# Attention with beacon keys and a gated MLP on one core: the order of work on every engine read from a table instead of made by a list schedule

## The chip, the cores and the metric

One core of a Trainium2 chip runs the whole program. Its engines are TensorE (PE, matrix products), VectorE (DVE), ScalarE (ACT), GpSimd (POOL) and SyncE (SP); each works through its own queue in order, and waits on semaphores for the others. Loads are issued from POOL, SP and ACT, stores from SP. The metric is the time of one execution on the device in microseconds. Before the change the median of 7 runs is 331.64 us (331.56 to 332.11).

## The reference

For 8 batches of 8 heads, 576 queries of width 64 attend to 16 beacon keys, which all may see, and to the keys up to their own place. The results of the 8 heads stand side by side as 4608 rows of 512, and go through an MLP of width 2048.

```python
k_all = np.concatenate([beacon_k, k], axis=2)
v_all = np.concatenate([beacon_v, v], axis=2)
scores = scale * np.matmul(q, k_all.transpose(0, 1, 3, 2))
causal[:, Nb:] = np.triu(np.ones((S, S), dtype=bool), k=1)
scores = np.where(causal, -1000000000.0, scores)
a = np.exp(scores - scores.max(-1, keepdims=True))
a /= a.sum(-1, keepdims=True) + 1e-09
attn_out = np.matmul(a, v_all)
x = attn_out.transpose(0, 2, 1, 3).reshape(B * S, H * D)
h = x @ w_in
out = (h * (1.0 / (1.0 + np.exp(-1.702 * h)))) @ w_out
```

## The kernel before

**Attention.** The work is cut into 16 sets, each of 4 heads of one batch. A set's queries and keys are loaded from POOL (`e_load_qk`, L373), its beacon keys from SP (`e_load_bk`, L408; for set 0 two of the four loads come from ACT) into one tile `bkf` that holds the beacon keys of all sets. VectorE casts a set's beacon keys (`e_bk`, L414, called `bk` and the set's number in the plan) and turns keys and queries with its 32 by 32 transpose (`e_turn`, L422 for the beacon part, L429 for the rest; `turn` in the plan). TensorE makes scores in chunks of 512 columns for 4 heads (`e_qk`, L458), all in one PSUM tile `s`, so that a chunk waits for the exp of the one before it (L469 on ScalarE). The causal edge is masked by POOL (L490), for the first two sets by VectorE (L483). Sums of the exps are taken by products with ones (`e_av` with x = 2, the sums product, L545; from set 4 on VectorE first adds the blocks up, `e_zadd`, L508), then transposed and inverted (L557, L564, L568: the "pair" z1 and z2), and the products with the values (L545, x = 0 and 1) are multiplied by the inverse into `xT` (`e_norm`, L580).

**MLP.** Rows come in groups: two of 256, eight of 512. The first product (`e_m1`, L604) fills one bank of 512 columns; the first two groups get their gate by tanh on ScalarE and a VectorE step (L618, L637), the others by one ScalarE step (L625), whose function table differs from exp's, so that ScalarE loads a table at each change. The second product of groups 2 to 9 is made of seven half-size products instead of eight (L718); VectorE prepares their operands (L669) and joins them (L734), and SP stores.

**Buffers.** Four PSUM banks form a ring for first products, second products and attention products. A bank is free again when the step that reads it (`closes`) has ended.

**Beacon loads after the first two sets.** The rest of `bkf` is filled in three parts, sets 2 and 3, 4 to 7, 8 to 15. For each part VectorE clears its slots (memset, L1086), and four loads on SP wait for that memset.

**The plan.** No instruction is issued where the code describes it. Each step is an `Op` with an engine, a length, and the ops that it depends on; `plan.run()` orders them, and the instructions are emitted in that order (L1103 to L1105). The program has semaphore waits for the true dependences, and no times: an engine does what is next in its queue as soon as its waits end. Before, `run` is a list schedule over those lengths: it takes the engine that can start first, and picks by priority, due time and a choice rule for TensorE (`choose`), with quotas for when a first-product group may start (`QUOTAS`), and due times for loads, turns and casts (`T_ATT0`, `T_ATT1`, `TDUE`). For a beacon load the plan counts 2500 ns from issue to landing:

```python
elif o.name == "bk" and o.eng != "DVE":
    lat = 2500
```

## Time and profile before

| | |
|---|---|
| median of 7 runs | 331.64 us |
| profiled execution | 331.86 us |
| its span, first to last instruction | 330.2 us |
| granted TensorE clock | 0.999 |
| TensorE busy | 311.1 us, 94% |
| VectorE, ScalarE, POOL busy | 237.9, 203.7, 115.5 us |
| first and last matmul | 8.60 us, 326.3 us |

The busy time of TensorE counts matmuls that overlap each other once. The strip below it in the page gives the busy share of 40 slices of 8.3 us. In the tables of groups and in the timeline, the number in brackets after an instruction is the time that its engine stood idle before it, and what ended that. Times that carry a "start to start" are differences between the starts of matmuls that follow each other.

### The profile page before, as it was taken

To read this page: it belongs to the slowest core of one execution; us is meant where nothing else is said; L and a number is where in the kernel's file an instruction comes from. 1 tells how busy PE (TensorE), PEld (TensorE's weight loads), DVE (VectorE), ACT (ScalarE), POOL (GpSimd) and SP (SyncE) were. 2 spreads that over 40 slices of the span, in tenths; PEclk is the share of its full clock that TensorE was granted. 3 is DMA by queue.
4 is the path that set the end of the run, shared out by engine and by line. 5 is a ranking of instruction groups with operands and counts; after the bars stand their busy time and mean duration, and the time that the engine had idled before them with its cause. 6 is when DMAs were issued, how large, how long until landed. Compare 5 with 4: busy or idle time off the path is not lost. (4 is left out here: it accounts for less than half of the span.)

```text
span 330.2 us, 9837 instructions
## 1 busy us (share of the span) xinstructions
PE 311.1 (94%) x4288; PEld 210.6 (64%) x4288; DVE 237.9 (72%) x478; ACT 203.7 (62%) x234; POOL 115.5 (35%) x178
## 2 busy tenths in 40 slices
PE   0699899999999999999999999999999999999995
PEld 0476566545885467646878877447774664746884
DVE  3847959796998788987999589978896630460484
ACT  1585487787767786777758586858677426175000
POOL 8765557372238205360427046702422000000000
PEclk9999999999999999999999999999999999999999
DMA  7999999669017903392149624930020000110122
GB/s 125 161 202 210 201 178 148 94 105 131 25 44 136 148 2 78 93 129 50 41 101 127 87 50 90 128 83 2 34 96 3 2 32 2 45 51 2 66 96 95
DMA packets 58219, 28.81 MB, mean 87 GB/s; under 512 B 41280, under 2 KB 53568, under 8 KB 58176
## 3 DMA queue, kind: packets, MB, share of 16 engines
q0 software_dynamic: 47552, 18.49, 48.1%
q1 hardware_dynamic: 10560, 9.69, 8.9%
q8 instruction: 33, 0.54, 0.7%
q14 instruction: 10, 0.08, 0.1%
q10 hardware_dynamic: 64, 0.01, 0.0%
HBM read 37.22 MB, written 9.44 MB: 141 GB/s over the span
## 5 line engine op out<-in xcount | busy, mean ns | idle before, releaser
L604 PE MATMUL u<-xT,w 128*128 128x512 f16 (+1 forms) x704 | 130.5, 342 | 2.4 <-DVE g L637 1.1
L469 ACT ACTIVATE E<-s 128x2048 f16<-128x2048 f32 (+4 forms) x66 | 98.8, 1514 | 42.8 <-PE s L458 42.1
L604 PEld LDWEIGHTS <-w 128*128 128x128 f16 x704 | 67.6, 98 | 59.1 <-issue 3.7
L625 ACT ACTIVATE g<-u 128x512 f16<-128x512 f32 x128 | 74.4, 599 | 43.2 <-PE u L604 43.1
L490 POOL TENSOR_SCALAR_AFFINE_SELECT E<-E 128x512 f16<-128x512 f16 (+3 forms) x78 | 50.7, 672 | 120.5 <-ACT E L469 116.8
L734 DVE SCALAR_TENSOR_TENSOR osb<-u,osb 128x512 f32<-128x512 f32 x56 | 37.4, 679 | 40.5 <-PE u L718 26.9
L718 PEld LDWEIGHTS <-g 128*128 128x128 f16 x512 | 48.7, 98 | 7.3 <-issue 0.2
L458 PE MATMUL s<-qT,kT 32*128 32x32 f16 (+20 forms) x1376 | 35.7, 234 | 12.0 <-DVE qT L429 8.6
L718 PE MATMUL u<-w,g 128*128 128x256 f16 x384 | 46.0, 273 | 0.0
L458 PEld LDWEIGHTS <-kT 32*128 32x128 f16 x1376 | 26.1, 95 | 29.0 <-issue 14.8
L718 PEld LDWEIGHTS <-sA 128*128 128x128 f16 x384 | 36.4, 98 | 4.9
L718 PE MATMUL u<-tB,sA 128*128 128x256 f16 x256 | 31.3, 273 | 0.0
L389 POOL DMA_DIRECT2D vb<-in_v_dram x32 | 27.3, 870 | 2.9 <-DMA kn<-in_k_dram 1.5
L545 PE MATMUL u<-E,vb 128*32 128x352 f16 (+8 forms) x928 | 27.7, 267 | 0.0
L580 DVE TENSOR_TENSOR xT<-u,rz 128x352 f16<-128x352 f32 (+2 forms) x52 | 24.8, 517 | 1.7 <-PE u L545 1.1
L508 DVE TENSOR_TENSOR zs<-zs,E 128x1344 f16<-128x1344 f16 (+2 forms) x36 | 23.2, 645 | 2.7 <-DVE zs L508 0.5
L545 PEld LDWEIGHTS <-vb 128*32 128x32 f16 (+1 forms) x928 | 20.1, 98 | 5.4 <-issue 1.3
L429 DVE STREAM_TRANSPOSE kT<-kn 128x576 f32<-128x576 f32 x16 | 20.1, 1258 | 4.7 <-PE s L458 2.8
L429 DVE STREAM_TRANSPOSE qT<-qn 128x576 f32<-128x576 f32 x16 | 20.0, 1247 | 3.7 <-DMA qn<-in_q_dram 1.9
L669 DVE TENSOR_TENSOR sA<-g 128x512 f16<-128x512 f16 x32 | 12.8, 417 | 12.4 <-ACT g L625 12.0
L557 DVE STREAM_TRANSPOSE zt<-u 128x352 f32<-128x352 f32 (+2 forms) x32 | 13.8, 459 | 7.8 <-PE u L545 7.6
L718 PE MATMUL u<-tB,g 128*128 128x256 f16 x128 | 16.3, 273 | 0.0
(44 smaller groups left out, 229.6 us busy)
## 6 DMA issues: line engine op xcount, KB each, us to landing
out_dram<-osb SPq DMA_DIRECT2D x36, 256.0 KB, 2.2
kn<-in_k_dram POOLq DMA_DIRECT2D x16, 288.0 KB, 6.3
qn<-in_q_dram POOLq DMA_DIRECT2D x16, 288.0 KB, 6.7
vb<-in_v_dram POOLq DMA_DIRECT2D x24, 128.0 KB, 5.6
w<-in_moe_w_in_dram POOLq DMA_DIRECT2D x8, 256.0 KB, 9.5
w<-in_moe_w_out_dram POOLq DMA_DIRECT2D x4, 512.0 KB, 14.0
vb<-in_v_dram POOLq DMA_DIRECT2D x8, 112.0 KB, 3.6
vb<-in_v_dram POOLq DMA_DIRECT2D x8, 80.0 KB, 5.4
```

The source lines that it names most:

```text
L389: nc.gpsimd.dma_start(out=t[0 : hi - lo, j, h0:h1, :], in_=v[b, h0:h1, lo:hi, :].rearrange("h n d -> n h d"),)
L429: nc.vector.transpose(out=f32(dst.rearrange("p n e -> p (n e)")).rearrange("p (r t) -> p t r", t=TR), in_=f32(src[:, :]).rearrange("p (t c ...
L458: nc.tensor.matmul(sc[:, h, o : o + w], kT[s % NB2][r : r + 32, j * P : (j + 1) * P, d], qT[s % NB2][r : r + 32, a : a + w, d], start=(d = ...
L469: nc.scalar.activation(out=Es[s][:, :, c0:c1], in_=ss[i][:, :, o : o + c1 - c0], func=AFT.Exp, scale=0.125,)
L490: nc.gpsimd.affine_select(out=blk, in_=blk, compare_op=ALU.is_ge, fill=0.0, base=off + (Nb if j == 0 else 0), pattern=[[0, Q], [1, w]], ch ...
L508: nc.vector.tensor_tensor(out=t, in0=E[:, :, Z0:S] if i == 1 else t, in1=E[:, :, wcol[i] : wcol[i] + S - a], op=ALU.add,)
L545: nc.tensor.matmul(u[32 * h : 32 * h + 32, a:e], lhs, src[0:kw, h, col : col + e - a], start=first, stop=last,)
L580: nc.vector.tensor_tensor(out=xT[:, 2 * hs + x : 2 * hs + x + n, t0 : t0 + w], in0=rings[("av", s, x, half)][:, 0 : n * w].rearrange("p (n ...
L604: nc.tensor.matmul(u[:, o + a - t0 : o + e - t0], w1t[:, kp, nt * P : (nt + 1) * P], xT[:, kp, a % XR : (e - 1) % XR + 1], start=(kp == 0) ...
L625: nc.scalar.activation(out=gts[g][:, n0:n1, 0:w], in_=rings[("m1", g, n0)][:, 0 : n * w].rearrange("p (n w) -> p n w", n=n), func=AFT.Gelu ...
L718: nc.tensor.matmul(u[:, HM * mt : HM * (mt + 1)], lhs[:, n, mt * P : (mt + 1) * P], rhs[:, n, :], start=(n == 0 and mt == 0), stop=(n == H ...
L734: nc.vector.scalar_tensor_tensor(out=osbs[(g, dst)][:, :], in0=rings[("p", g, p)][:, :], scalar=scale_of(g), in1=osbs[(g, src)][:, :], op0 ...
```

## The change

The list schedule is gone, with its rules, quotas and the two constants `NEAR` and `IDLE`. In its place stands a table `ORDER` with one row for each engine and one for the DMA queue of POOL: the numbers of the ops, in the order in which they were described in the code, written down in the order in which the engine is to do them. `run` takes each row from its head, and works out starting times from the same kind of lengths and latencies, only to assign ring banks and to emit the rows in one common order. Due times and priorities are still written at the ops, and nothing reads them any more. Some dependences are added to the plan (a transpose of sums waits for the inverse two before it; VectorE's additions wait for the sums products two sets before; a tanh waits for the tanh before it and for a gate three before); they name buffers that are reused. The planned length of VectorE's additions goes from 0.517 to 0.6 ns per element. The ops themselves, what each issues, are as before.

The table is cut here to the heads of four rows. In them 73 and 97 are the beacon casts of sets 0 and 1; 74 and 75 the turns of set 0's keys and queries, 98 and 99 those of set 1; 82 is the memset for sets 2 and 3, 83 to 86 are its four loads, 224 is the cast of set 2, and 225 and 226 are its turns; 126 and 128 are norms of set 0's second half; on TensorE 76, 100, 106, 108 are score chunks 0 to 3, 145 the sums product of set 1's second half, 176 the first step of a second product.

```diff
-NEAR = 500
-IDLE = 800
+ORDER = {
+    "PE": [
+        76, 100, 115, 118, 120, 106, 138, 143, 141, 108, 152, 111, 155, 158, 129, 161, 122, 164, 131, 167, 170, 134,
+        127, 125, 173, 176, 145, 148, 150, 177, 182, 188, 191, 227, 194, 197, 183, 232, 203, 200, 234, 178, 179,
...
+    "DVE": [
+        73, 97, 74, 75, 98, 99, 78, 81, 80, 116, 117, 102, 121, 104, 105, 119, 139, 140, 144, 142, 154, 157, 123,
+        124, 82, 160, 166, 163, 169, 172, 224, 126, 128, 175, 146, 147, 149, 151, 225, 226, 87, 190, 193, 196, 255,
...
+    "SP": [
+        0, 2, 4, 5, 6, 7, 83, 84, 85, 86, 88, 89, 90, 91, 181, 93, 94, 95, 96, 187, 217, 223, 348, 364, 371, 377,
...
     def run(self):
-        free = {e: 0 for e in ("PE", "ACT", "DVE", "POOL", "Q", "SP")}
+        todo = {e: [self.ops[i] for i in seq] for e, seq in ORDER.items()}
+        free = {e: 0 for e in todo}
         free.update(POOL=900, SP=700)
...
+        while any(todo.values()):
+            n = len(order)
+            for e, seq in todo.items():
+                k = 0
+                for o in seq:
+                    if any(d.end is None for d in o.deps):
+                        break
+                    t = max([free[e]] + [d.end + self.lat(d, o) for d in o.deps])
...
+                    o.start, o.end = t, t + dur
+                    free[e] = o.end
+                    order.append(o)
+                    k += 1
+                del seq[:k]
...
+    def lat(self, d, o):
+        if o.eng == "Q":
+            return 300 if d.eng == "SP" else 1200
+        if d.name == "bk" and d.eng != "DVE":
+            return 2500
+        return self.LAT[d.eng] if o.eng != d.eng or d.eng == "Q" else 0
...
-    QUOTAS = (19, 28, 38, 42, 48, 55, 55, 55)
...
-    T_ATT0, T_ATT1 = 17000, 249000
+    T_ATT0, T_ATT1 = -1000, 245000
...
+            deps += [avs.get((s - 2, 2, h)) for h in range(2)] if s - 2 >= EARLY else []
...
-    SQ, SDVE, TDUE = 2, 0, 60000
+    SQ, SDVE, TDUE = 2, 0, 75000
```

## The prediction

> **What bounds the kernel now.** I read the page first, then the stretch-by-stretch table, the list of waits, the timeline of the first 14 us and the view of the beacon-key tile `bkf`.

> ```profile
> PE 311.1 (94%) x4288; PEld 210.6 (64%) x4288; DVE 237.9 (72%) x478; ACT 203.7 (62%) x234; POOL 115.5 (35%) x178
> ...
> PE   0699899999999999999999999999999999999995
> ```

> TensorE is the bound: one empty slice at the start, one half-empty at the end, nearly full between. It starts its first matmul at 8.60 us and ends its last at 326.3; a join and a store close the span of 330.2. So a new order can win only what TensorE stands still. Where that is, stage by stage (PE busy is the first number after the length):

> ```profile
> 33.00:66.00 33.00, 31.29 (x582) 19.85 (x584) 25.77 (x45) 22.70 (x22) 18.23 (x30) 1.00 1.22 155
> 66.00:99.00 33.00, 32.54 (x435) 21.30 (x428) 28.82 (x54) 24.99 (x28) 13.71 (x19) 1.00 0.55 76
> 99.00:132.00 33.00, 32.30 (x465) 20.26 (x463) 27.07 (x56) 24.47 (x28) 14.37 (x22) 1.00 0.66 91
> ...
> 198.00:231.00 33.00, 32.24 (x442) 20.47 (x440) 28.66 (x56) 23.60 (x28) 13.30 (x18) 1.00 0.55 76
> ```

> Idle: 1.71 + 0.46 + 0.70 + 0.76, with 0.32 in 16.5 to 33, is 3.95 us; the other stages from 132 to 314 show none. A wait is partly covered by the tail of the matmul before it: counted from start to start of matmuls, against undisturbed neighbours of the same kind, the loss after 20 us is 5.8 us in 17 places. That is the most that the middle can give. What ends these waits:

> ```profile
> PE s L458 <- ACT E L469: 3.4, 4, 2.0
> ...
> PE u L604 <- DVE g L637: 1.1, 1, 1.1
> ...
> PE u L604 <- ACT g L625: 1.0, 3, 0.4
> ```

> The three waits for `g` are the entries into first-product groups 2, 3 and 6. One of them:

> ```profile
> 66.53 1.88 ACT L469 ACTIVATE E<-s 128x2048 f16<-128x2048 f32 x1 [0.79 <-PE s L458]
> ...
> 68.42 1.28 ACT L625 ACT_TABLE_LOAD   x1
> ...
> 70.37 1.89 PE L604 MATMUL u<-xT,w 128*128 128x512 f16 x8 [0.35 <-ACT g L625]
> ```

> TensorE fills the four ring banks in 3.5 us, while ScalarE needs 1.88 + 1.28 + 0.60 before the first bank is free.

> The start is a chain of its own:

> ```profile
> 3.79 0.20 DVE L414 CAST bkn<-bkf 128x64 f16<-128x64 f32 x1 [2.56 <-DMA bkf<-in_beacon_k_dram]
> ...
> 5.63 1.26 DVE L429 STREAM_TRANSPOSE kT<-kn 128x576 f32<-128x576 f32 x1 [1.40 <-DMA kn<-in_k_dram]
> ...
> 7.29 1.26 DVE L429 STREAM_TRANSPOSE qT<-qn 128x576 f32<-128x576 f32 x1 [0.40 <-DMA qn<-in_q_dram]
> ...
> 8.60 1.04 PE L458 MATMUL s<-qT,kT 32*128 32x288 f16 x24 [8.60 <-DVE qT L429]
> 8.67 0.19 DVE L414 CAST bkn<-bkf 128x64 f16<-128x64 f32 x1
> ...
> 10.24 1.23 DVE L429 STREAM_TRANSPOSE qT<-qn 128x576 f32<-128x576 f32 x1
> ...
> 11.68 1.04 PE L458 MATMUL s<-qT,kT 32*128 32x288 f16 x24 [2.04 <-ACT E L469]
> ```

> VectorE turns the keys and queries of set 0 as they land, TensorE starts 0.05 us after the second turn; only then, at 8.67, comes the beacon cast of set 1. When did the data of that cast land? The `bkf` view, first over the window of SP's last load of set 1, then over the four loads of sets 2 and 3:

> ```profile
> L408 SPq DMA_DIRECT2D bkf<-in_beacon_k_dram x1: 443/443/443, 3.3 to 3.3; - x1
> ...
> DMA to landing us min/median/max: 5.2/5.2/5.2
> ```

> ```profile
> L408 SPq DMA_DIRECT2D bkf<-in_beacon_k_dram x4: 328/460/542, 12.4 to 13.9; - x4
> ...
> DMA to landing us min/median/max: 5.4/5.5/6.0
> ```

> Set 1's beacon keys are complete at 3.3 + 5.2 = 8.5 us, and a beacon load of 4 to 8 KB takes 5 to 6 us, not the 2.5 us that the planner's latency rule gives it (`lat` in the new code, the same number in the old loop). The four loads of sets 4 to 7, issued at 29.6, took 5.5 to 6.5.

> [...] here the start-to-start excess at a change is 0.09 to 0.12 us.

> **The change, part by part.** The instructions are the same but for ScalarE's table loads; what moves is their order, so the bill is start, waits, changes of mode.

> *Start (A).* VectorE's row of the table begins 73, 97, 74, 75: the cast of set 1 (97) stands ahead of both turns of set 0 (74, 75). It waits for all four loads of set 1, so for 8.5 us; SP and POOL issue the same loads in the same order before that, so the landing does not move. Behind it stand the turns, and TensorE behind them. From the cast on, the sequence is that which the trace shows for set 1: cast at 8.67, last turn from 10.24 for 1.23, and 0.05 to the matmul: 11.5 instead of 8.60, **+2.9**. The next score chunk follows the exps of the first (9.69 + 1.94, then 0.05), so it shifts by the same, and so does all that hangs on it; the weights have landed by then, which only removes a wait (counted in C). Bounds: +2.4 if the later steps find slack, +3.0.

> *Sets 2 and 3 (B).* The memset of their `bkf` slots (82), which their loads (83 to 86, SP) wait for, ran at 12.23 and its cast (224) at 28.26, long after landing (13.9 + 5.4 = 19.3). The table puts 82 behind the reciprocal pair of set 0's second half, and 224 six places later. Old times: the sums product at 24.85, its transpose at 25.58, pair done at 26.9. The new TensorE order has that product ahead of a first-product tile pair and a score chunk (1.5 us), so at 24.85 - 1.5 + 2.9 = 26.2; pair and memset done 2.1 later, 28.3; first load 0.1 later; last issue 1.5 after it, 29.9; landing 5.4 after that: about 35.3. VectorE has only five gates in between and then stands at the cast; behind it are the two norms (126, 128) that free ring banks, and TensorE's next product (av 1.2.1) needs the first: 35.3 + 0.2 + 0.45 + 0.05 = 36.0. TensorE gets there, by the old durations of the ten steps since 26.2 (7.1 us), at 33.3. **+2.6**; 1.5 if the loads land in 4.3 us, 3.7 with the 6.5 of the later group. The loads of sets 4 to 7, moved likewise, have by the same count some 8 us from the last issue to their first cast: nothing, while they land in under 8.

> *Waits won (C).* The 1.1 us gate wait stood behind three turns, in the table behind two: -1.0. Groups 2 and 3 are entered with three tiles, a score chunk, then the fourth: the 0.6 us chunk covers their 0.5 each; group 6 keeps 0.1 of 0.5: -1.4. The waits of score chunks for exps at 65.8 and 102.4 (0.4 each), the weight wait at 27 and the norm wait at 34 (0.8), others near 86 to 101 and 164 to 168 (0.7): -2.3. Against them I take +0.8 for places where the new order leaves no slack (chunk 8 behind its turn, sums products behind VectorE's additions near 125 and 204), and 0.9 as a haircut, since every wait removed leaves the next one closer. **-3.0**; from -4.2 to -1.5.

> *Changes of mode and table (D).* 147 changes against 145: **+0.2**. The built program has 14 table loads for 12: 2 x 1.28 on ScalarE, busy 62%, hidden by TensorE's other work; up to +1 if one stands at a group entry.

> Sum against the profiled execution (331.86, span 330.2): 2.9 + 2.6 - 3.0 + 0.2 = +2.7, span 332.9. The median of the runs shown is 331.64, 0.2 under that execution: **334.3**.

> **Rivals.** *Faster:* the loads of sets 2 and 3 land early. They are issued 16 us later than before, perhaps into emptier queues; the third group, issued at 29.6, took longer, which speaks against it. Below 3 us to landing B is nothing, C can then be had in full (-4.2): 331.64 + 2.9 - 4.2 + 0.2 = 330.5. It decides only if both hold: with C at -3.0 the start alone eats it. *About even:* only B falls away, because TensorE is late itself or the norms come by another path: 331.7. *Worse:* landing takes 6.5 us (B 3.7) and C is only -1.5: 336.9. *The table is not what runs* is excluded: the built program has 97 ahead of 74.

> **How the numbers follow.** The stated case 0.61, its own range 333.0 to 335.6; worse 0.17; about even 0.13; faster 0.09. Measurement can tell 0.2% (331.0 to 332.3) from no change. Even splits half and half between same and slower, so same 0.07, and a little of the faster case ends within the bound too: faster 0.08, same 0.08, slower 0.84. Range 332.0 to 336.5 leaves out the faster case, a part of the even one and the top of the worse.

> **What would show it.** A: the first matmul at 11.5, VectorE's second cast at 8.6 with an idle before it ended by a DMA of `bkf`. B: VectorE idle 3 to 5 us ahead of a cast between 30 and 36, and TensorE 2 to 3 us idle ended by a norm. C: less than 3 us of other TensorE idle after 40 us, no wait for `g` at the group entries. Wrong if the first matmul stays before 9, or if that cast does not wait.

## The result and the profile after

The kernel with the table takes **334.71 us** in the median of 13 runs (332.90 to 336.44), beside 331.75 us of the kernel before on the same chip (33 runs, 331.32 to 333.05). The ratio is 1.0089, with a 95% interval of 1.0073 to 1.0105: about 0.9% slower. The prediction said 334.3 us, slower, between 332.0 and 336.5. The profiled execution of after took 336.11 us, its span 334.4 us, so it is one of the longer ones; why there are longer ones is a finding of this study.

Line numbers of after are those of before less 24 (the scores are L434, the first product L580, the score exps L445, the casts L390, the turns L405).

The page of after, first the engines, then the strips of 40 slices:

```profile
PE 312.5 (93%) x4288; PEld 212.0 (63%) x4288; DVE 234.8 (70%) x478; ACT 201.2 (60%) x236; POOL 112.7 (34%) x178
...
PE   0399699999999999999999999999999999999995
...
PEclk9999799999999999999999999999999999999999
```

Two marks stand in the same slice, the fifth (33 to 42 us): TensorE is only 60% busy there, and the clock granted to it falls. The second slice (8.4 to 16.7 us) has a 3 where before it had a 6. The rest is full. In numbers, counted from start to start of matmuls against undisturbed neighbours of the same kind:

| TensorE | before, us | after, us | difference |
|---|---|---|---|
| first matmul | 8.60 | 11.35 | +2.75 |
| lost from there to 24 us | 6.52 | 6.85 | +0.33 |
| lost in 24 to 60 us | 2.06 | 4.86 | +2.80 |
| of that: one gap at 34 us | none | 3.33 | +3.33 |
| of that: three slow stretches of matmuls after it | none | 1.35 | +1.35 |
| of that: all other waits | 2.06 | 0.18 | -1.88 |
| lost after 60 us | 3.52 | 1.46 | -2.06 |
| end of last matmul | 326.31 | 330.54 | +4.23 |

Of the 6.52 and 6.85 us lost up to 24 us only 2.7 and 2.8 are idle time; most of the rest lies in matmuls that are slower at the start (numbers at the end). The parts add up to 2.75 + 0.33 + 2.80 - 2.06 = 3.82; the 0.4 that is left contains the changes of tiling mode (147 for 145; in the trace of before one costs 0.09 to 0.12 us from start to start, so 0.2 for the two) and what the method cannot resolve.

**The start.** The timeline of after, VectorE and TensorE alone (start, duration, engine, line, operation; in brackets the idle before it and what ended it):

```profile
3.44 0.20 DVE L390 CAST bkn<-bkf 128x64 f16<-128x64 f32 x1 [2.20 <-DMA bkf<-in_beacon_k_dram]
...
8.61 0.19 DVE L390 CAST bkn<-bkf 128x64 f16<-128x64 f32 x1 [4.98 <-DMA bkf<-in_beacon_k_dram]
8.72 0.20 DVE L398 STREAM_TRANSPOSE kT<-bkn 128x32 f32<-128x32 f32 x1
8.96 1.25 DVE L405 STREAM_TRANSPOSE kT<-kn 128x576 f32<-128x576 f32 x1
...
10.06 1.23 DVE L405 STREAM_TRANSPOSE qT<-qn 128x576 f32<-128x576 f32 x1
...
11.35 1.04 PE L434 MATMUL s<-qT,kT 32*128 32x288 f16 x24 [11.35 <-DVE kT L398]
```

VectorE stands 4.98 us at the cast of set 1. The keys and queries of set 0 land meanwhile: before, the turn of the keys began at 5.63 and that of the queries was done at 8.55. The first matmul follows the turn as before.

**Sets 2 and 3.** Timeline of after:

```profile
28.43 0.17 DVE L1072 MEMSET bkf<- 128x128 f32 x1
...
28.63 1.73 SPq L384 DMA_DIRECT2D bkf<-in_beacon_k_dram  x4
...
36.41 0.65 DVE L390 CAST bkn<-bkf 128x64 f16<-128x64 f32 x1 [4.48 <-DMA bkf<-in_beacon_k_dram]
36.52 0.81 DVE L556 TENSOR_TENSOR xT<-u,rz 128x288 f16<-128x288 f32 x2
37.14 1.15 PE L521 MATMUL u<-E,ones 128*32 128x288 f16 x20 [3.26 <-DVE xT L556]
```

Memset, loads, landing at 36.3, cast, norm, TensorE: each waits for the one ahead of it, as the prediction has it. The loads of this profile took 4.4 to 6.4 us to land, median 4.7 (view of the tile `bkf`).

**After the gap.** The stretches of after around it (length, then busy time of PE, PEld, DVE, ACT, POOL, each with the number of its instructions, then the granted clock of TensorE, DMA share and GB/s):

```profile
34.00:37.20 3.20, 0.06 (x4) 0.06 (x7) 0.79 (x3) 0.00 (x0) 3.20 (x5) 0.91 1.20 204
37.20:41.00 3.80, 3.80 (x65) 2.58 (x65) 3.08 (x9) 0.00 (x0) 1.13 (x2) 0.63 1.52 191
41.00:45.00 4.00, 4.00 (x52) 2.99 (x51) 3.71 (x5) 1.79 (x3) 0.00 (x0) 1.00 2.14 173
```

The clock record of the trace has half clock from 36.60 for 3.41 us. That gives what is seen here: 0.60 us at half in the first stretch (1 - 0.30 / 3.20 = 0.91), 2.81 us in the second (1 - 1.405 / 3.80 = 0.63), none in the third. So after a gap of 3.3 us TensorE works for 2.9 us (37.14 to 40.01) at half clock in this execution. This the prediction did not have.

**What was won.** In the table of groups the first product now hardly waits, and the stretch from 60 us to 120 us, in which TensorE stood 1.54 us before, has 0.14 us left. Before, then after:

```profile
L604 PE MATMUL u<-xT,w 128*128 128x512 f16 (+1 forms) x704 | 130.5, 342 | 2.4 <-DVE g L637 1.1 <-ACT g L625 1.0 <-issue 0.3
...
60.00:120.00 60.00, 58.46 (x817) 35.17 (x814) 52.01 (x100) 45.60 (x54) 25.41 (x38) 1.00 0.66 88
```

```profile
L580 PE MATMUL u<-xT,w 128*128 128x512 f16 (+1 forms) x704 | 131.4, 342 | 0.1
...
60.00:120.00 60.00, 59.86 (x922) 36.19 (x911) 50.37 (x94) 45.57 (x50) 26.72 (x43) 1.00 0.75 103
```

### The profile page after: what moved, and what is told of

Read it like the earlier page. It is cut to its first block, busy times and chain, and to the rows that moved or that the text cites. A ratio compares the mean times of both kernels' runs of the same rounds, so it can differ in the third digit from the quotient of the medians.

```text
span 334.4 us, 9823 instructions
## 1 busy us (share of the span) xinstructions
PE 312.5 (93%) x4288; PEld 212.0 (63%) x4288; DVE 234.8 (70%) x478; ACT 201.2 (60%) x236; POOL 112.7 (34%) x178
## 3 DMA queue, kind: packets, MB, share of 16 engines
q1 hardware_dynamic: 10560, 9.69, 8.9%
## 5 line engine op out<-in xcount | busy, mean ns | idle before, releaser
L580 PE MATMUL u<-xT,w 128*128 128x512 f16 (+1 forms) x704 | 131.4, 342 | 0.1
L445 ACT ACTIVATE E<-s 128x2048 f16<-128x2048 f32 (+4 forms) x66 | 98.9, 1514 | 46.8 <-PE s L434 46.4
L580 PEld LDWEIGHTS <-w 128*128 128x128 f16 x704 | 67.8, 98 | 53.5 <-issue 0.8
L601 ACT ACTIVATE g<-u 128x512 f16<-128x512 f32 x128 | 69.8, 599 | 46.1 <-PE u L580 45.9
L466 POOL TENSOR_SCALAR_AFFINE_SELECT E<-E 128x512 f16<-128x512 f16 (+3 forms) x78 | 48.1, 643 | 128.2 <-ACT E L445 119.3
L694 PE MATMUL u<-w,g 128*128 128x256 f16 x384 | 49.3, 273 | 0.0
L434 PE MATMUL s<-qT,kT 32*128 32x32 f16 (+20 forms) x1376 | 35.9, 234 | 14.3 <-DVE kT L398 11.3
L434 PEld LDWEIGHTS <-kT 32*128 32x128 f16 x1376 | 26.2, 95 | 31.2 <-issue 13.1
L694 PE MATMUL u<-tB,sA 128*128 128x256 f16 x256 | 34.3, 273 | 0.0
L521 PE MATMUL u<-E,vb 128*32 128x352 f16 (+8 forms) x928 | 28.9, 273 | 0.0
L556 DVE TENSOR_TENSOR xT<-u,rz 128x352 f16<-128x352 f32 (+2 forms) x52 | 25.9, 519 | 3.2 <-PE u L521 2.5
L521 PEld LDWEIGHTS <-vb 128*32 128x32 f16 (+1 forms) x928 | 21.1, 101 | 6.0 <-issue 1.7
L405 DVE STREAM_TRANSPOSE kT<-kn 128x576 f32<-128x576 f32 x16 | 20.1, 1256 | 3.2 <-PE s L434 1.9
L484 DVE TENSOR_TENSOR zs<-E 128x1856 f16<-128x1856 f16 x12 | 15.4, 1283 | 9.4 <-POOL E L466 9.4
L533 DVE STREAM_TRANSPOSE zt<-u 128x224 f32<-128x224 f32 (+2 forms) x32 | 14.8, 472 | 7.7 <-PE u L521 7.6
L405 DVE STREAM_TRANSPOSE qT<-qn 128x576 f32<-128x576 f32 x16 | 19.8, 1235 | 0.0
```

What stands on the lines that cost most here:

```text
L405: nc.vector.transpose(out=f32(dst.rearrange("p n e -> p (n e)")).rearrange("p (r t) -> p t r", t=TR), in_=f32(src[:, :]).rearrange("p (t c ...
L434: nc.tensor.matmul(sc[:, h, o : o + w], kT[s % NB2][r : r + 32, j * P : (j + 1) * P, d], qT[s % NB2][r : r + 32, a : a + w, d], start=(d = ...
L445: nc.scalar.activation(out=Es[s][:, :, c0:c1], in_=ss[i][:, :, o : o + c1 - c0], func=AFT.Exp, scale=0.125,)
L466: nc.gpsimd.affine_select(out=blk, in_=blk, compare_op=ALU.is_ge, fill=0.0, base=off + (Nb if j == 0 else 0), pattern=[[0, Q], [1, w]], ch ...
L484: nc.vector.tensor_tensor(out=t, in0=E[:, :, Z0:S] if i == 1 else t, in1=E[:, :, wcol[i] : wcol[i] + S - a], op=ALU.add,)
L521: nc.tensor.matmul(u[32 * h : 32 * h + 32, a:e], lhs, src[0:kw, h, col : col + e - a], start=first, stop=last,)
```

## The experiments

**Theories.** *A and B:* two moved casts, that of set 1 and that of set 2 with its late memset, cost about 2.5 us each, and the rest of the table wins about 3. *Rivals:* the time is lost somewhere else, in the changed lengths and added dependences or in places without slack that the table makes all over; or one of the two casts is all of it, because the other is hidden. Seven of the ten kernels are a table with its numbers in another order and nothing else changed; the three of experiments 6 to 8 add work. None leaves anything out of the computation.

**1. Cast of set 1 behind the turns of set 0, as before the change (A undone).**

```diff
     "DVE": [
-        73, 97, 74, 75, 98, 99, 78,
+        73, 74, 75, 97, 98, 99, 78,
```

> Table of the change with one move: the cast of set 1 (97) stands behind both turns of set 0 again (73, 74, 75, 97, 98). Theory (two casts wait for beacon loads, each on the path): first matmul at 8.6 us instead of 11.35, all later work 2.75 us earlier, the cast of set 2 waits as before: 334.7 - 2.75 = 332.0 (331.3 to 332.6), and the runs stay as widely spread as those of the change. Rival (the late start is absorbed further on, because loads or the next cast set the pace): first matmul at 8.6 but the time within 0.8 us of 334.7, with a longer wait at the cast of set 2.

Measured: 332.20 us (330.19 to 335.05, 14 runs), ratio to before 1.0013 (0.9989 to 1.0036). The first matmul is back at 8.52 us, and the end of the last one comes at 326.8. That is 2.5 us less than after: A is confirmed, in place and size. The gap of B is still there, 3.2 us long in the profiled execution:

```profile
33.83 0.20 DVE L386 CAST bkn<-bkf 128x64 f16<-128x64 f32 x1 [4.48 <-DMA bkf<-in_beacon_k_dram]
33.94 0.82 DVE L552 TENSOR_TENSOR xT<-u,rz 128x288 f16<-128x288 f32 x2
...
34.45 0.68 PE L517 MATMUL u<-E,ones 128*32 128x288 f16 x20 [3.14 <-DVE xT L552]
```

The wide spread, which the prediction did not have, is here too, as expected for this run. Sorted by the mean clock of each run the times part: 330.19 to 332.36 at 0.998 and more (8 runs), 333.18 to 333.79 at 0.994 to 0.995 (5 runs), 335.05 at 0.990 (1 run). In the profiled execution above the clock stayed full, and the same 20 matmuls that took 1.15 us in after took 0.68. After's own runs part in the same way: 332.90 to 334.71 at 0.997 and more (7 runs), 335.51 to 336.44 at 0.994 to 0.995 (6 runs). Compared group by group, A is worth 2.9 us (333.70 - 330.83) at the full clock and 2.8 (336.06 - 333.27) at the lower one, close to the 2.75 of the first matmul.

**2. Cast of set 2 directly ahead of its turns, behind the two norms (the wait of B undone, the late memset kept).**

```diff
-        124, 82, 160, 166, 163, 169, 172, 224, 126, 128, 175, 146, 147, 149, 151, 225, 226,
+        124, 82, 160, 166, 163, 169, 172, 126, 128, 175, 146, 147, 149, 151, 224, 225, 226,
```

> Table of the change with one move: the cast of set 2 (224) stands directly ahead of set 2's turns (225), eight places later; its loads are issued as in the change. Theory: the norms no longer stand behind the cast, TensorE's 3.3 us before the products of set 1's second half go, and with them the slower matmuls after that gap (1.4 us in the profile): first matmul at 11.35, time 331.75 + 2.75 - 3.2 = 331.3 (330.6 to 332.2), runs within 1 us of each other. Rival (the gap only moves to the turns of set 2, where chunk 8 then waits for the same landing): 333.5 or more. Rival (the slower matmuls come from elsewhere): they stay, 332.7.

Measured: 332.02 us (331.51 to 332.75, 21 runs), ratio 1.0005 (0.9999 to 1.0012). The gap is gone, the mean clock is at least 0.997 in every run, and the range is 1.2 us instead of 3.5. That is 2.7 us less than after. It ends at the upper edge of what was expected: two waits of TensorE that after does not have appear, 0.74 us of a score chunk for its turn at 39.7 and 0.24 us of a first product. The data of set 1 landed later in this profile, so that its first matmul comes at 11.76 us.

**3. Both (A and B undone): what the rest of the table is worth.** Edits 1 and 2 together.

> Both moves of the two runs above, the rest of the table as in the change. Theory (the rest of the table is better than the list schedule by the waits it takes away): before less 3.2, 331.75 - 3.2 = 328.6 (327.9 to 329.4), faster than the kernel before. Rival (the new order of the middle brings nothing, and only looks so beside the two waits): 331.0 to 332.5. Rival (TensorE earlier by 6 us runs into loads of keys, values and weights that are no earlier): 329.5 to 331.

Measured: 330.02 us (329.55 to 330.26, 5 runs), ratio 0.9942 (0.9930 to 0.9954). The table without the two casts is faster than the list schedule, but by 1.8 us, where 3.2 were expected; the time lies in the range of the second rival. The timeline shows where TensorE stands:

```profile
36.67 0.64 PE L430 MATMUL s<-qT,kT 32*128 32x288 f16 x24 [0.42 <-DVE qT L401]
...
40.19 0.56 POOL L345 DMA_DIRECT2D kn<-in_k_dram  x1 [2.42 <-DMA w<-in_moe_w_out_dram]
40.38 1.43 DVE L386 CAST bkn<-bkf 128x64 f16<-128x64 f32 x1
...
40.75 1.49 POOL L462 TENSOR_SCALAR_AFFINE_SELECT E<-E 128x512 f16<-128x512 f16 x3
...
41.72 0.68 DVE L609 SCALAR_TENSOR_TENSOR g<-sig,u 128x512 f16<-128x512 f16 x1
...
42.45 1.03 PE L576 MATMUL u<-xT,w 128*128 128x256 f16 x8 [0.76 <-DVE g L609]
```

The cast of set 3, not touched by the edit, takes 1.43 us instead of 0.2 beside POOL's work; the gate step behind it is late, and with it a first product. With 0.5 for the score chunk at 36.67 and 0.24 for another product, start to start these waits cost 0.49 + 0.24 + 0.93 = 1.66 us. The second rival is right in part: POOL comes late to its masks because it stood 2.42 us for a load of weights; the two smaller waits are ended by VectorE alone.

In after none of the three is seen. The longest, 0.93, is gone in every kernel whose TensorE comes to this place 2 us or more later, by A, by B or by clears (experiments 1, 2, 4 and 6 to 8): there POOL is no longer late for its masks, and the cast takes 0.47 to 0.48 us. The two smaller ones remain with the gap of B at full clock (0.35 and 0.24 in experiment 1) and with A alone (0.74 and 0.24 in experiment 2); in after the matmuls ahead of them run at half clock, so that VectorE is in time. So B costs less than its gap and the half clock together: taking it out brings back 0.98 us of waits beside A, and 1.66 without A.

**4. The memset of sets 2 and 3 early, the cast where the table has it (the cause of B removed at its other end).**

```diff
-        119, 139, ... 124, 82, 160,
+        119, 82, 139, ... 124, 160,
```

> Table of the change with another single move: the memset (82) that the loads of sets 2 and 3 wait for stands eight places earlier, ahead of the transpose of set 1's first sums, so that these loads start some 9 us earlier; the cast of set 2 stays where the change has it. Theory (it is the landing that the cast waits for, not the cast's own place): the same as with the cast moved, 331.3 (330.6 to 332.2), no idle ahead of that cast. Rival (the place of the cast ahead of the norms costs by itself, or the earlier loads land no earlier): 333 or more.

Measured: 331.63 us (331.30 to 332.83, 13 runs), ratio 0.9999 (0.9991 to 1.0007). No gap at 30 to 40 us. The cast alone, ahead of the norms, harms nothing when its data are there: B needs the late loads *and* the early cast. Either of the two repairs it (332.0 and 331.6).

**5. As 3, with the cast of set 3 behind the gate step.** This tests whether the slow cast causes the wait of 0.93 us in experiment 3.

```diff
-        190, 193, 196, 255, 199,
+        190, 193, 196, 199, 255,
```

> The table with both casts moved back (330.0), and one more move: the cast of set 3 (255) stands behind the next gate (199). In the run with both moves that cast took 1.43 us from 40.38 on, while GpSimd worked, against 0.18 elsewhere, and TensorE waited 0.9 us for the gate behind it. Theory (what is missing to the 3.2 us that the rest of the table was to bring lies largely here): TensorE's wait near 42.4 goes, 330.0 - 0.9 = 329.1 (328.6 to 329.6). Rival (the wait comes from the gates or banks themselves and only moves): 329.8 to 330.3.

Measured: **329.42 us** (329.20 to 329.80, 5 runs; before 331.81), ratio 0.9930 (0.9917 to 0.9942). The product of 16 matmuls now runs in one piece, and the cast, still slowed, holds up nobody:

```profile
40.73 1.92 PE L576 MATMUL u<-xT,w 128*128 128x256 f16 x16
...
41.06 0.61 DVE L386 CAST bkn<-bkf 128x64 f16<-128x64 f32 x1
```

Three casts moved make the table 0.7% faster than the kernel before. The step from experiment 3, 0.6 us, is small beside the spread of five runs each, whose ranges overlap. In this profile the score chunk at 36.76 waits 1.05 us, twice as long as in experiment 3, so not all of the 0.93 us comes through. A new search over the table with the landing times of the trace was not tried.

**6 to 8. How long must TensorE stand before its clock falls?** In the table of experiment 3 VectorE is given N clears of a tile that nothing needs at that time, ahead of the norm (126) where B's cast stood: extra work, no wait for a load, a gap of a set length in the same place. In the clock record of after the full clock ahead of the gap lasts 4 times 3.413 us, the half clock once that, the full clock behind it 86 times; one such stretch is called a window.

```diff
 def e_norm(...):
+    for _ in range(N if (s, x, half) == (0, 0, 1) else 0):
+        nc.vector.memset(tB[0][:, :, :].bitcast(F32), 0.0)
```

N = 3:

> The table with both casts moved back, with VectorE clearing an unused tile three times (about 2.75 us, extra work) ahead of the norm that TensorE's next product waits for; TensorE reached that place 1.26 us after the norm ended, so it stands about 1.5 us. Theory (TensorE's clock is halved for one window of 3.41 us after a window in which it mostly stood): no halved clock, 330.0 + 1.5 less what the gap absorbs of the waits near 37 to 42, so 330.5 to 331.5, runs within 1 us. Rival (any gap halves the clock): 1.4 us more than that.

N = 5:

> As the short gap, with five clears (about 4.5 us), so that TensorE stands about 3.3 us, as in the change itself. Theory: the gap is near the length of one window, so it depends on where the windows lie whether one is empty enough: runs fall into two groups about 1.4 us apart, 331.5 to 332.3 with the mean clock at 0.997 or above and 333.0 to 333.8 with 0.994 to 0.995. Rival (the spread of the change came from the landing of its loads, which nothing here waits for): one group within 0.8 us.

N = 7:

> As the short gap, with seven clears (about 6.4 us), so that TensorE stands about 5.1 us. Theory: some window is always empty or nearly so, the clock is halved in every run, mean clock 0.994 or lower, 330.0 + 5.1 - 1.4 absorbed + 1.4 for the slow window = 335.1 (334.2 to 336.0), runs within 1 us or, where a second window is caught, 1.7 us more. Rival (the halved clock has another cause than the gap): mean clock 0.997 or above, 333.3 to 334.0.

| N | gap of TensorE, us | median, us | range, runs | mean clock of the runs |
|---|---|---|---|---|
| 0 (experiment 3) | none | 330.02 | 329.55 to 330.26, 5 | at least 0.998 |
| 3 | 1.95 | 331.17 | 330.23 to 331.80, 20 | at least 0.997 |
| 5 | 4.33 | 334.03 | 334.00 to 335.04, 5 | 0.995 three times, 0.990 twice |
| 7 | 6.71 | 336.66 | 336.21 to 336.92, 4 | 0.989 to 0.990 |

From one clear to the next it took 1.19 us (0.91 of work and 0.28 between), longer than planned, so N = 5 gave 4.33 us of gap where 3.3 were meant. It missed its expectation (two groups between 331.5 and 333.8) for that reason, and did not show a gap of B's length; experiment 1 and after do. N = 7 came out above its range: its gap was 1.6 us longer than the 5.1 meant. Its clock fell for two windows (6.83 us), and TensorE still stood for most of the first. The stretches of N = 5, then those of N = 7:

```profile
32.00:36.00 4.00, 1.15 (x38) 1.08 (x41) 3.44 (x7) 0.00 (x0) 2.38 (x4) 0.95 1.13 207
36.00:40.00 4.00, 4.00 (x41) 2.02 (x31) 3.34 (x9) 0.00 (x0) 1.47 (x3) 0.62 1.26 207
```

```profile
32.00:36.00 4.00, 0.00 (x0) 0.00 (x0) 3.05 (x4) 0.00 (x0) 2.51 (x3) 0.84 1.12 206
36.00:40.00 4.00, 2.56 (x52) 2.04 (x55) 3.37 (x8) 0.00 (x0) 1.60 (x2) 0.50 1.25 205
40.00:44.00 4.00, 4.00 (x36) 2.28 (x25) 3.81 (x7) 0.23 (x1) 0.56 (x1) 0.81 2.27 164
```

At N = 5 the clock record has half clock for 3.41 us from 35.62, at N = 7 for 6.83 us from 34.69, twice that: one window and two. From N = 0 to N = 3 a gap of 1.95 costs 1.15 us in the median. The trace of N = 3 shows why it is less: the wait of 0.93 is gone, with the cast at 0.48 us, while the score chunk still waits 0.54 us and the other product 0.16 (idle times). From 3 to 5 another 2.38 of gap costs 2.86, from 5 to 7 another 2.38 costs 2.63: more than the gap itself, once the clock falls.

**9. A alone on the old order.** The order of the list schedule of before, written down as a table of the same form, with only the cast of set 1 (97) ahead of 74 and 75. It also tests the rival that the table form, the new lengths or the added dependences cost anything by themselves.

> The order of the list schedule, written as a table, with one part of the change alone: the cast of set 1 (97) ahead of the turns of set 0 (74). Theory (the start is a chain that nothing later absorbs): first matmul at about 11.4 us, 331.8 + 2.75 = 334.6 (333.9 to 335.0), less about 0.4 where the late start covers the wait for weights near 27 us. Rival (the step is absorbed, as the two moves together suggest, where the late cast cost 2.0 rather than 2.75): 333.2 to 333.8.

Measured: 334.46 us (334.44 to 334.50, 5 runs; before 331.86), ratio 1.0077 (1.0063 to 1.0091). The first matmul starts at 11.28, VectorE waits just as in after:

```profile
8.55 0.20 DVE L377 CAST bkn<-bkf 128x64 f16<-128x64 f32 x1 [4.95 <-DMA bkf<-in_beacon_k_dram]
```

One number moved by two places costs +2.6 us. The first matmul moved by 2.68, so nothing is left for the form of the table, the lengths or the dependences.

**10. The group entries put back (a part of C undone).** Experiment 3 with the score chunk (435, 610) behind the fifth tile instead of the third on entering first-product groups 2 and 3.

```diff
     "PE": [
-        312, 292, 306, 435, 308, 316,
+        312, 292, 306, 308, 316, 435,
...
-        488, 504, 498, 610, 494, 516,
+        488, 504, 498, 494, 516, 610,
```

> The table with both casts moved back (330.0), with one part of the middle undone: in the first products of groups 2 and 3 the score chunk that stands after the third tile stands after the fifth, as the list schedule entered them with four tiles in a row. Theory (these entries are part of what the table wins): a wait of about 0.5 us for the first g in each, 330.0 + 1.0 = 331.0 (330.5 to 331.4). Rival (the entries do not matter, since the tiles' waits are made up in the same group): 329.8 to 330.3.

Measured: 330.79 us (330.55 to 330.97, 5 runs), ratio 0.9966 (0.9954 to 0.9979), 0.8 above experiment 3. The waits of before are back at their places, 0.57 us start to start at 70.3 and 0.51 at 106.7:

```profile
68.35 1.28 ACT L592 ACT_TABLE_LOAD   x1
...
70.29 1.02 PE L571 MATMUL u<-xT,w 128*128 128x512 f16 x4 [0.41 <-ACT g L592]
```

The chunk pulled ahead covers this wait behind the table load of 1.28 us. It is the only step of C that was tried alone.

## Why the prediction was right

The direction, the two mechanisms and their places are as forecast, and the time lies 0.4 us from the forecast one. That it is so close is in part luck: B cost more than forecast, C brought more than forecast beside B, and the median falls between two groups of runs. By its steps:

- **A, +2.9: right.** First matmul forecast at 11.5, seen at 11.35 (+2.75 against before). In the median 2.5 (after less experiment 1), 2.6 (experiment 9 less before) and 2.0 (experiment 2 less 3, where 0.7 us of experiment 3's waits are gone). The landing of 8.5 us, read off one DMA row, held in after and in experiment 9, where the cast came at 8.61 and 8.55 us; in experiments 2 and 4 it came at 9.02 and 9.32, and the first matmul at 11.76 and 12.06. So the landing moved by some 0.8 us over these four executions, and with it all that waited for it.
- **B, +2.6: mechanism right, two terms missing.** Memset at 28.43 (28.3 forecast), last issue begun at 29.93 (29.9), landing 36.3 (35.3; the last load took 6.4 us instead of 5.4), gap 3.33 (2.6). In the median B is worth 2.7 (after less experiment 2), 3.1 (after less experiment 4) or 2.2 (experiment 1 less 3). Two terms were not in the sum, and they work against each other: the half clock behind the gap, +1.35 in the profiled execution, and the waits that come back without B, 0.98 in experiment 2 and 1.66 in experiment 3. That they leave B near its forecast size is luck.
- **C, -3.0: in its range, for a mixed reason.** In after the waits fell by 1.88 + 2.06 and rose by 0.33 at the start, -3.6. The deduction of 0.9 and the 0.8 of new waits were too much for after. Without B they were right: experiment 3 is 1.8 below before, so C with D is only -1.8 (experiment 5: -2.4). The prediction took B and C as independent, and they are not. For the entries of groups 2 and 3 it counted 0.5 each; experiment 10 gives 0.8 for both.
- **D, +0.2:** ScalarE is busy 2.5 us less than before in spite of two more table loads; nobody in after waits for them at a group entry. What two more changes of mode cost was not tried by itself, so the +0.2 stays an estimate (two of 0.09 to 0.12 us, from the trace of before).
- **Sum.** It gave +2.7 against the profiled execution of before; the profiled execution of after has +4.25 (336.11 - 331.86), of which 1.35 is the half clock. The 7 runs of after with full clock have a median of 333.7, the 6 others 336.1. The forecast of 334.3 lies between, as does the median. That the two groups lie 2.4 apart, not 1.35, would fit a later landing and a longer gap in the second, but neither the gap of unprofiled runs nor the end of their slow start is known, and that stays open.
- **Rivals.** "About even" (only B falls away) would have been 331.7; it is what experiments 2 and 4 measured, at 332.0 and 331.6, by removing B. "Faster" needed loads that land in under 3 us; they took 4.4 to 6.4. "Worse" had the right landing time for the last load, 6.4, but needed a small C. A loss elsewhere is not seen: with A and B undone the table is faster than the list schedule.

## What to carry to other kernels

An order judged by planned lengths is as good as its worst length. Two casts stood ahead of work that was ready, and as VectorE took its queue in order, each held up TensorE by 2 to 3 us (2.75 and 3.33). How the table was found is not known, but the planned times that `run` works out show how the cost stays hidden. With its 2.5 us for a landing (4.4 to 6.4 measured), the first score chunk is planned at 8.72 us with the table's cast of set 1 and at 8.48 with the cast behind the turns, the sums product behind the norms at 29.80 either way, and the whole program even ends 0.14 us earlier with both casts as the table has them. With 5.5 in place of 2.5, and nothing else changed, it is planned to end 4.4 us later with them. Read from the trace when data land, and keep an instruction that waits for a load behind everything on its engine that is ready by then; here it cost two or three numbers in a table.

And the effects of an order did not add here. A stall changed what met what further on: that of B hid waits (0.98 us came back without it in experiment 2, 1.66 in experiment 3), and the matmuls behind it were slowed by 1.35 us at half clock. So what its removal brought was not its length.

## What was not expected of the hardware

```profile
33.19:36.60 3.41, 0.69 (x4) 0.19 (x2) 0.19 (x2) 0.46 (x1) 3.41 (x5) 1.00 1.19 206
36.60:40.01 3.41, 2.87 (x60) 2.23 (x59) 2.83 (x8) 0.00 (x0) 1.43 (x3) 0.50 1.28 202
```

```profile
29.40:32.81 3.41, 1.91 (x20) 1.17 (x13) 0.00 (x0) 1.09 (x2) 1.96 (x4) 1.00 1.16 209
32.81:36.22 3.41, 1.77 (x61) 1.56 (x61) 2.32 (x7) 0.00 (x0) 2.34 (x3) 1.00 1.13 206
36.22:39.64 3.42, 3.42 (x24) 2.16 (x23) 3.28 (x6) 0.60 (x1) 0.98 (x2) 1.00 1.25 209
```

```profile
30.84:34.26 3.42, 1.54 (x40) 1.11 (x42) 3.14 (x6) 0.35 (x1) 2.21 (x4) 1.00 1.12 209
34.26:37.67 3.41, 3.41 (x50) 2.23 (x42) 3.17 (x8) 0.00 (x0) 2.32 (x3) 1.00 1.19 205
```

In the window ahead TensorE was busy 20% in after, 56 and then 52% in experiment 1, 45% in N = 3. Counted over all twelve traces, behind the slow start, half clock followed each of the 16 windows in which TensorE was busy 30% or less (most of them at the end of the kernel; 1% in before, 20 and 12% in after) and none with 45% or more (69% is the next in before, 84% in after); between 30 and 45% no window was seen, and where the fall begins is not shown. So the gap of 3.3 us in after was followed by half clock and that of 3.2 us in experiment 1 was not, each in one execution. In timed runs the clock fell (mean of 0.995 or less) in 6 of 13 of after and 6 of 14 of experiment 1, never in the 20 with a gap of 1.95 us, always with 4.33 and 6.71. How much of the half-and-half of B's kernels comes from where the gap lies and how much from its length, which moves with the landing, is not known: both gaps were measured in one execution each, and no run sets the edges. Of the 3.41 us at half clock in after 0.54 passed while TensorE still stood; the price was 1.35 us of the matmuls behind the gap: the 20 of a sums product took 1.15 us instead of 0.68.

**The start is slow too, and the mean clock does not tell.** The clock records have their first entry, full clock, between 15.56 and 24.61 us in the twelve traces. Before it matmuls are slower: in after, whose first entry lies at 22.95 us, 8 of a first product took 1.94 us from 20.66 on; behind it 16 took 1.92 from 23.18 on, and 8 took 1.05 from 25.50 on. What has no entry counts as full in the mean clock of a run, so this can be part of the spread of runs that all show 0.997 and more; that was not tested.

**VectorE's small cast was often slower beside POOL.** In before and after it took 0.17 to 0.19 us with nothing of POOL's beside it; it took 0.65 in after while POOL issued loads, 0.61 and 1.43 in experiments 5 and 3 while POOL masked. Of the 192 casts in the twelve traces 70 took more than 0.25 us, up to 1.51, and 65 of these ended within 0.1 us after an instruction of POOL had ended (in before and after 11 of 32, and all 11 ended 0.02 to 0.06 us after one); but 52 others stood beside work of POOL and took 0.25 or less, as that at 8.61 us of after with 0.19. What the slow casts waited for is not shown: no run separated it. The wait on the path in experiment 3 was 0.93 us.
